# Four larger gaps of attention work per unit instead of eight, in a fused RWKV-7 and mixture-of-experts kernel

## The chip, the cores and the metric

One core of a Trainium2 chip. The metric is the device time of one execution in microseconds (us). The engines are called as in the profile: PE is TensorE's matmul, PEld its weight load, DVE VectorE, ACT ScalarE, POOL GpSimd, SP SyncE.

## The reference, cut to what matters

```python
# attention: batch 4, heads 8, 768 tokens, head size 40, float32
for t in range(S):
    y[:, :, t]  = einsum('bhd,bhde->bhe', r_t, state)
    Sa          = einsum('bhde,bhe->bhd', state, a_t)
    state       = state * w_t - einsum('bhd,bhe->bhde', Sa, b_t) + einsum('bhd,bhe->bhde', v_t, k_t)
# x = y as (3072 tokens, 320); then 4 experts of 320 -> 1024 -> 320
p = domain_probs / (domain_probs.sum(-1, keepdims=True) + 1e-9)
for e in range(4):
    out += p[:, e:e+1] * (relu(x @ w1[e]) @ w2[e])
```

## The kernel before

The kernel works on 24 units: one unit is 64 tokens of two batches with all 8 heads. The recurrence over tokens is turned into small matrices inside a unit. Four generators make the attention of a unit, and each `yield` is a place where the driver may put other work on TensorE: `within` (does not need the state: `pw`, `pg`, transposes of A, N, K, R, V, `pc`, `pf`, `pe`, `pev`), `substitute` (a triangular solve of 31 steps on GpSimd), `merge` (`pY`, `pQ`), and `step` (`prh`, `psn`, `psa`, `pst`, `px`, `prs`, `psd`, `py`). The mixture of a unit is four "ups" (`ph`) and four "downs" (`po`). An up contracts 320 features: two blocks of 128 rows and one of 64.

Two rings of PSUM banks matter: four banks for everything small, four for the mixture. A bank is a piece of the memory that TensorE writes, and it is written anew only after its last reader: in the kernel before, the third `psn` matmul starts at 633.91 us, 0.06 after the copy of `pQ` has ended (633.85). Four names besides those of the banks come back below: `gl` is the product of a unit's decays and reads `pw`, EV is the copy of `pev`, QTc is the result of the substitution, which `pY` needs, and `xT` is the input of the mixture, which a transfer brings from the result of `py`. The profile records a float32 matmul twice and a transpose once (18724 records: 9024 matmuls twice, 676 transposes once); the counts of matmuls below are counts of records.

```python
def big(name):
    return ps.tile([P, 512], FP32, name=name, tag="big", bufs=4)

def within(q):
    pw = by(turn("pw", tok(n["W"]))[:], L)                 # 4 transposes into one bank
    nc.scalar.copy(out=G[:, :, 1:L], in_=pw[:, :, 0:L - 1])
    nc.vector.tensor_tensor_scan(out=G[...], ...)          # running product of the decays
    nc.vector.tensor_tensor(out=q.gl[:], in0=pw[:, :, L - 1:L], in1=G[:, :, L - 1:L], op=ALU.mult)
    yield
    ... # pg; RT, VT, pc; AT, NT, KT; pf, pe; pev: a yield after each group

def up(e):
    ph = [ps.tile(..., tag="mm", bufs=4) for _ in range(2)]
    for f in range(NF):                # 128-row blocks first: 32 records
        for g in range(2): ...         # lhsT=w1_sb[:, e, g, ...], rhs=xT[:, g, :]
    for f in range(0, NF, 2):          # then the 64-row block: 16 records
        for i in range(2): ...         # lhsT=w1_last[...], rhs=xT[i * DT:(i + 1) * DT, 2, :]
    # Relu on ScalarE

for n, stages in enumerate(((before, s), (s,), (s,), (s, m, w), (w,), (w,), (w,), (w, m))):
    for gen in stages:
        next(gen, None)
    ...
    mix(1)                             # one up or one down after each of eight small gaps
```

The order of the program text is not quite the order on TensorE, because the framework's scheduler moves instructions: in the trace of the changed kernel unit 1's `pY` starts at 73.89 us, ahead of unit 0's first up (76.34), which the text has before it.

Of the kernel before, what the change touches and what calls it, by code (L numbers as in the profile page):

```python
# [15 lines left out]
def kernel(  # L16
# [51 lines left out]
    def big(name):  # L68
        return ps.tile([P, 512], FP32, name=name, tag="big", bufs=4)
# [203 lines left out]
    def within(q):  # L273
# [3 lines left out]
        q.G = G = sb.tile([P, 2 * NJ, L], FP32, name="G", tag="G", bufs=2)  # L277
# [6 lines left out]
        q.gl = sb.tile([P, 2 * NJ, 1], FP32, name="gl", tag="gl", bufs=3)  # L284
# [8 lines left out]
        nc.vector.reciprocal(out=gp[:], in_=gp[:])  # L293
        q.K, q.N = k_tok(), n_tok()
# [5 lines left out]

        def turned(name, x, keep=False):
            t = sb.tile([P, NJ, P], FP32, name=name, tag=name if keep else "turned", bufs=2)
            nc.scalar.copy(out=t[:].rearrange("p j t -> p (j t)"), in_=turn("p" + name, tok(x))[:])  # L303
            return t

        def causal_scores():
            q.RT = turned("RT", n["R"], True)
            VT = turned("VT", q.V)
            q.CT = causal(CTs(), quadrants("pc", BY_TOKENS, L, lambda j, s, i: (
                d_half(j, s), i, j, of_pairs(VT, d_half(j, s), j, i), of_pairs(q.RT, d_half(j, s), j, i),  # L310
            )))

        if not q.start:
            causal_scores()
# [5 lines left out]
        yield  # L320

# [11 lines left out]
        if q.start:  # L333
            causal_scores()
# [10 lines left out]
    def substitute(q, eng):  # L345

        blocks = sb.tile([P, H, Q], FP32, name="blocks", bufs=2)
# [158 lines left out]
    def mixture(q, xT):  # L506
# [4 lines left out]
        def up(e):  # L511
            ph = [ps.tile([P, NF // 2, P], FP32, name="ph", tag="mm", bufs=4) for _ in range(2)]

            for f in range(NF):
                for g in range(2):
                    nc.tensor.matmul(  # L516
                        out=ph[f % 2][:, f // 2, :], lhsT=w1_sb[:, e, g, f * P:(f + 1) * P],
                        rhs=xT[:, g, :], start=(g == 0 and f < 2), stop=False,
                    )
            for f in range(0, NF, 2):  # L520
                for i in range(2):
                    nc.tensor.matmul(  # L522
                        out=ph[i][:, f // 2, :], lhsT=w1_last[i * DT:(i + 1) * DT, e, f // 2, :],
                        rhs=xT[i * DT:(i + 1) * DT, 2, :], start=False, stop=(f == NF - 2),
                    )
            for i in range(2):
                h = sb.tile([P, NF // 2, P], FP32, name="hs", tag="hs", bufs=6)
                nc.scalar.activation(out=h[:], in_=ph[i][:], func=ACTF.Relu)  # L528
                hs[e, i] = h

        def down(e):
            po = ps.tile([P, DM], FP32, name="po", tag="mm", bufs=4)
            for f in range(NF):
                nc.tensor.matmul(  # L534
                    out=po[:], lhsT=hs[e, f % 2][:, f // 2, :], rhs=w2_sb[:, e, f, :],
                    start=(f == 0), stop=(f == NF - 1),
                )
            sc = gate[:, q.c, q.bp, e:e + 1]
            if e == 0:
                nc.vector.tensor_scalar(out=osb[:], in0=po[:], scalar1=sc, scalar2=None, op0=ALU.mult)  # L540
            else:
                nc.vector.scalar_tensor_tensor(  # L542
                    out=osb[:], in0=po[:], scalar=sc, in1=osb[:], op0=ALU.mult, op1=ALU.add,
                )

        up(0)
        yield
        for e in range(E):
            if e + 1 < E:
                up(e + 1)  # L550
                yield
            down(e)
            yield
        for i in range(2):
            row = q.b[i] * S + q.c * L
            nc.sync.dma_start(out=out[row:row + L, :], in_=osb[i * L:(i + 1) * L, :])

    work = []

    def mix(n):  # L560

        while n and work:
            try:
                next(work[0])
                n -= 1
            except StopIteration:
                work.pop(0)
# [10 lines left out]
    for u in (0, 1, 1, 1):  # L578
# [4 lines left out]
    m = merge(units[0])  # L583
    run(m, 2)
    for u in range(NU):
        q = units[u]
        xT = sb.tile([P, 3, P], FP32, name="xT", tag="xT", bufs=3)
        s = step(q, xT)
        w, before = iter(()), m
        more = u + 2 < NU  # L590
        if u + 1 < NU:
            m = merge(units[u + 1])
        if more:
            load(begin(u + 2), srcs)
            w = within(units[u + 2])
        for n, stages in enumerate(((before, s), (s,), (s,), (s, m, w), (w,), (w,), (w,), (w, m))):
            for gen in stages:
                next(gen, None)
                if u == 0 and n == 3 and gen is s:
                    for e in range(2, E):  # L600
                        load_expert(e)
                    run(z)
            if n == 3:
                work.append(mixture(q, xT))
            if n == 6 and more:
                run(substitute(units[u + 2], nc.gpsimd))
            if u or n % 2:
                mix(1)
    mix(-1)


# [26 lines left out]
```

## Time and profile before

| | before |
|---|---|
| time, median of 4 | 1244.37 us (1243.86 to 1245.14) |
| TensorE busy | 1197.9 us, 96% |
| next busiest | GpSimd, 41% |
| one unit in the steady part, `pw` to `pw` | 49.73 us (median of the trace) |
| units | 24 |

TensorE is full from the fourth slice on, so the time is a prologue plus some twenty equal units. The lines that show this stand in the prediction. This is the timeline of TensorE in the kernel before from the first up of unit 0; the columns are start, length, engine, line, operation, result and sources, array shape, operand shape, count, and in brackets an idle time and what ended it.

```profile
63.54 0.68 PE L516 MATMUL ph<-xT,w_sb 128*128 128x128 f32 x4
...
66.25 3.36 PE L516 MATMUL ph<-xT,w_sb 128*128 128x128 f32 x28 [0.71 <-DMA xT<-Y]
69.54 1.16 PE L522 MATMUL ph<-xT,w_last 64*128 64x128 f32 x16
...
72.97 0.70 PE L233 MATMUL pKT<-ident,k_tok 128*128 128x128 f32 x4 [1.79 <-DVE Z L366]
73.47 5.36 PE L516 MATMUL ph<-xT,w_sb 128*128 128x128 f32 x32
78.76 1.16 PE L522 MATMUL ph<-xT,w_last 64*128 64x128 f32 x16
...
83.25 0.69 PE L390 MATMUL pY<-QTc,F 32*32 32x32 f32 x32
```

The first up of unit 0 fills most of the time in which VectorE works on unit 1's substitution (its last Z ends at 73.0); the second follows, and `pY`, whose input QTc is ready at 74.3, comes only at 83.25.

### The profile page before, as it was taken

To read this page: it belongs to the slowest core of one execution; us is meant where nothing else is said; L and a number is where in the kernel's file an instruction comes from. 1 tells how busy PE (TensorE), PEld (TensorE's weight loads), DVE (VectorE), ACT (ScalarE), POOL (GpSimd) and SP (SyncE) were. 2 spreads that over 40 slices of the span, in tenths; PEclk is the share of its full clock that TensorE was granted. 3 is DMA by queue.
4 is the path that set the end of the run, shared out by engine and by line. 5 is a ranking of instruction groups with operands and counts; after the bars stand their busy time and mean duration, and the time that the engine had idled before them with its cause. 6 is when DMAs were issued, how large, how long until landed. Compare 5 with 4: busy or idle time off the path is not lost.

```text
span 1241.6 us, 42664 instructions
## 1 busy us (share of the span) xinstructions
PE 1197.9 (96%) x18724; PEld 1012.1 (82%) x18724; DVE 382.7 (31%) x790; ACT 319.6 (26%) x801; POOL 505.7 (41%) x1668
## 2 busy tenths in 40 slices
PE   5389999999999999999999999999999999999998
PEld 4378888888888888888888888888888888888886
DVE  5543143142231431422314314223143142231110
ACT  3122322222223222222232222222222222222111
POOL 4434634526426345264263452643634526436000
PEclk9699999999999999999999999999999999999999
DMA  5772220120211201202112012021120220000000
GB/s 97 173 199 49 35 45 13 35 45 9 40 30 18 46 13 35 44 10 39 26 23 45 12 36 42 11 40 24 24 45 12 36 42 11 14 14 2 13 13 6
DMA packets 179176, 45.55 MB, mean 37 GB/s; under 512 B 159488, under 2 KB 177968, under 8 KB 178992
## 3 DMA queue, kind: packets, MB, share of 16 engines
q1 hardware_dynamic: 177872, 42.66, 17.7%
q8 instruction: 148, 2.42, 0.8%
q10 hardware_dynamic: 1120, 0.16, 0.1%
q14 instruction: 36, 0.29, 0.1%
HBM read 34.13 MB, written 3.93 MB: 31 GB/s over the span
## 4 chain that ended last, share of the span: by engine, by line
PE 93%; DVE 2%; POOL 1%; ACT 1%; issue 1%; DMA 0%; SPq 0%; DVEq 0%; ACTq 0%; POOLq 0%
PE po L534 34%; PE ph L516 29%; PE ph L522 8%; PE py L260 2%; PE psd L260 2%; ACT QT L407 1%; PE pQ L402 1%; PE psa L260 1%; PE pY L390 1%; PE px L260 1%; PE psn L260 1%; PE pf L260 1%; PE pev L260 1%; PE pc L260 1%; PE pw L233 1%
## 5 line engine op out<-in xcount | busy, mean ns | idle before, releaser
L534 PE MATMUL po<-w_sb,hs 128*128 128x320 f32 x1536 | 440.2, 437 | 0.0
L534 PEld LDWEIGHTS po<-w_sb,hs 128*128 128x128 f32 x1536 | 282.5, 190 | 107.3
L516 PE MATMUL ph<-xT,w_sb 128*128 128x128 f32 x3072 | 367.7, 278 | 0.7 <-DMA xT<-Y 0.7
L516 PEld LDWEIGHTS ph<-xT,w_sb 128*128 128x128 f32 x3072 | 352.3, 193 | 6.3 <-DMA xT<-Y 0.9
L360 POOL TENSOR_TENSOR tmp<-M,Z 128x60 f32<-128x60 f32 (+24 forms) x713 | 196.3, 275 | 94.1 <-DVE M L353 40.1
L366 POOL TENSOR_TENSOR Z<-Z,tmp 128x60 f32<-128x60 f32 (+24 forms) x713 | 202.3, 284 | 55.8
L528 ACT ACTIVATE hs<-ph 128x512 f32<-128x512 f32 x192 | 104.2, 595 | 416.4 <-PE ph L522 416.4
L349 POOL COPY blocks<-F 32x256 f32<-32x256 f32 x92 | 36.2, 393 | 309.8 <-ACT F L327 306.9
L542 DVE SCALAR_TENSOR_TENSOR osb<-po,gate,osb 128x320 f32<-128x320 f32 x72 | 39.6, 551 | 335.0 <-PE po L534 335.0
L383 POOL COPY QT<-QTc 32x256 f32<-32x256 f32 x96 | 54.0, 563 | 185.7 <-DVE QTc L377 182.0
L522 PE MATMUL ph<-xT,w_last 64*128 64x128 f32 x1536 | 111.6, 285 | 0.0
L522 PEld LDWEIGHTS ph<-xT,w_last 64*128 64x128 f32 x1536 | 93.2, 187 | 11.6
L268 DVE COPY_PREDICATED TT<-mask_up,pe 128x256 f32<-128x256 int32 x48 | 18.6, 439 | 147.8 <-PE pe L260 147.8
L540 DVE TENSOR_SCALAR osb<-po,gate 128x320 f32<-128x320 f32 x24 | 13.2, 550 | 161.9 <-PE po L534 161.9
L462 ACT COPY RS<-prs 64x256 f32<-64x256 f32 x88 | 32.2, 366 | 103.2 <-PE prs L260 102.1
L353 DVE STREAM_TRANSPOSE M<-blocks 128x1024 f32<-128x1024 f32 x24 | 47.3, 1971 | 33.7 <-POOL blocks L349 33.7
L293 DVE RECIPROCAL gp<-gp 128x320 f32<-128x320 f32 x24 | 51.4, 2142 | 0.0
L476 DVE TENSOR_TENSOR state<-psd,state 128x160 f32<-128x160 f32 x44 | 12.2, 319 | 118.6 <-PE psd L260 118.6
L303 ACT COPY AT<-pAT 128x512 f32<-128x512 f32 x24 | 14.0, 585 | 110.6 <-PE pAT L233 110.6
L407 ACT COPY QT<-pQ 32x256 f32<-32x256 f32 x48 | 17.4, 362 | 85.5 <-PE pQ L402 85.2
L303 ACT COPY RT<-pRT 128x512 f32<-128x512 f32 x24 | 14.0, 585 | 80.6 <-PE pRT L233 80.6
L390 PE MATMUL pY<-QTc,F 32*32 32x32 f32 x768 | 17.0, 194 | 15.6 <-DVE QTc L377 15.6
(114 smaller groups left out, 1139.5 us busy)
## 6 DMA issues: line engine op xcount, KB each, us to landing
w_sb<-in_moe_w_dram SPq DMA_DIRECT2D x4, 1280.0 KB
w_sb<-in_moe_w_dram SPq DMA_DIRECT2D x8, 512.0 KB
natW<-in_w_dram SPq DMA_DIRECT2D x48, 80.0 KB
natA<-in_a_dram SPq DMA_DIRECT2D x48, 80.0 KB
natB<-in_b_dram SPq DMA_DIRECT2D x48, 80.0 KB
natK<-in_k_dram SPq DMA_DIRECT2D x48, 80.0 KB
out_dram<-osb SPq DMA_DIRECT2D x48, 80.0 KB
xT<-Y SPq DMA_DIRECT2D x168, 20.0 KB
```

Source lines behind the costliest of these rows:

```text
L260: nc.tensor.matmul(out=p[row][half(col), at * out_cols:(at + 1) * out_cols], lhsT=lhsT, rhs=rhs, start=(n == 0), stop=(n == len(terms) - 1),)
L293: nc.vector.reciprocal(out=gp[:], in_=gp[:])
L349: ins = eng.tensor_copy(out=blocks[quarter(i)], in_=q.F[quarter(i), :, quarter(i % 2)])
L353: nc.vector.transpose(out=M[:], in_=cols)
L360: ins = eng.tensor_tensor(out=t, in0=M[:, j:j + 1, j + 1:Q].to_broadcast([P, n, m]), in1=Z[:, 0:n, j:j + 1].to_broadcast([P, n, m]), op=AL ...
L366: eng.tensor_tensor(out=Z[:, 0:n, j + 1:Q], in0=Z[:, 0:n, j + 1:Q], in1=t, op=ALU.add)
L383: ins = nc.gpsimd.tensor_copy(out=q.QT[quarter(i), :, quarter(i % 2)], in_=QTc[quarter(i)])
L516: nc.tensor.matmul(out=ph[f % 2][:, f // 2, :], lhsT=w1_sb[:, e, g, f * P:(f + 1) * P], rhs=xT[:, g, :], start=(g == 0 and f < 2), stop=False,
L522: nc.tensor.matmul(out=ph[i][:, f // 2, :], lhsT=w1_last[i * DT:(i + 1) * DT, e, f // 2, :], rhs=xT[i * DT:(i + 1) * DT, 2, :], start=Fals ...
L528: nc.scalar.activation(out=h[:], in_=ph[i][:], func=ACTF.Relu)
L534: nc.tensor.matmul(out=po[:], lhsT=hs[e, f % 2][:, f // 2, :], rhs=w2_sb[:, e, f, :], start=(f == 0), stop=(f == NF - 1),)
L542: nc.vector.scalar_tensor_tensor(out=osb[:], in0=po[:], scalar=sc, in1=osb[:], op0=ALU.mult, op1=ALU.add,)
```

## The change

Its intent: fewer and larger gaps, each with its transposes first, so that TensorE changes its array shape less often; and mixture pieces of one up and one down whose 64-row blocks come first, directly after the 64-row matmuls of attention.

```diff
-        return ps.tile([P, 512], FP32, name=name, tag="big", bufs=4)
+        return ps.tile([P, 512], FP32, name=name, tag="big", bufs=5)
@@ within: RT and VT are transposed one gap earlier, pc one gap later; gl gets 4 buffers, G gets 3
@@ mixture
-            ph = [... tag="mm", bufs=4 ...]
-            (32 records of 128 rows, then 16 of 64 rows)
+            ph = [... tag="mm", bufs=3 ...]
+            for f in range(0, NF, 2):
+                for i in range(2):
+                    nc.tensor.matmul(..., lhsT=w1_last[...], rhs=xT[i * DT:(i + 1) * DT, 2, :],
+                                     start=(f == 0), stop=False)
+            for f in range(NF):
+                for g in range(2):
+                    nc.tensor.matmul(..., rhs=xT[:, g, :], start=False, stop=(g == 1 and f >= NF - 2))
@@ the pieces of a unit: up(0), the last unit's down(3), up(1), down(0), up(2), down(1), up(3), down(2)
@@ driver, for each unit u
-        for n, stages in enumerate(((before, s), (s,), (s,), (s, m, w), (w,), (w,), (w,), (w, m))): ...
+        share = 1 + (u > 1)
+        run(w, 1); run(w_next); run(s, 1)        # C: pw; pev; px, prs
+        mix(share)
+        run(w, 1); run(s)                        # D: pg, RT, VT; psd, py
+        if u:
+            mixture(q, q.xT)
+        run(w, 1); run(m, 1)
+        mix(share)
+        run(w, 2); run(m, 1); run(s_next, 1); run(m)   # A: AT, NT, KT; pc, pY, prh, psn, pQ
+        mix(share)
+        run(w, 1); run(s_next, 1)                # B: pf, pe, psa, pst
+        mix(2 if u else 1)
```

A piece is one up or one down.

More of the change, by code (lines that the diff above doesn't have):

```diff
@@ L276, in within @@
         pw = by(turn("pw", tok(n["W"]))[:], L)
-        q.G = G = sb.tile([P, 2 * NJ, L], FP32, name="G", tag="G", bufs=2)
+        q.G = G = sb.tile([P, 2 * NJ, L], FP32, name="G", tag="G", bufs=3)
         nc.vector.memset(G[:, :, 0:1], 0.0)
@@ L283, in within @@
         )
-        q.gl = sb.tile([P, 2 * NJ, 1], FP32, name="gl", tag="gl", bufs=3)
+        q.gl = sb.tile([P, 2 * NJ, 1], FP32, name="gl", tag="gl", bufs=4)
         nc.vector.tensor_tensor(out=q.gl[:], in0=pw[:, :, L - 1:L], in1=G[:, :, L - 1:L], op=ALU.mult)
@@ L293, in within, with turned, turn_rv, causal_scores @@
         nc.vector.reciprocal(out=gp[:], in_=gp[:])
+        def turned(name, x, keep=False):
+            t = sb.tile([P, NJ, P], FP32, name=name, tag=name if keep else "turned", bufs=2 if keep else 3)
+            nc.scalar.copy(out=t[:].rearrange("p j t -> p (j t)"), in_=turn("p" + name, tok(x))[:])
+            return t
+        def turn_rv():
+            q.RT = turned("RT", n["R"], True)
+            return turned("VT", n["V"])
+        def causal_scores(VT):
+            q.CT = causal(CTs(), quadrants("pc", BY_TOKENS, L, lambda j, s, i: (
+                d_half(j, s), i, j, of_pairs(VT, d_half(j, s), j, i), of_pairs(q.RT, d_half(j, s), j, i),
+            )))
+        if not q.start:
+            VT = turn_rv()
+            yield
         q.K, q.N = k_tok(), n_tok()
@@ L299, in within @@
         q.V = n["V"]
-        def turned(name, x, keep=False):
-            t = sb.tile([P, NJ, P], FP32, name=name, tag=name if keep else "turned", bufs=2)
-            nc.scalar.copy(out=t[:].rearrange("p j t -> p (j t)"), in_=turn("p" + name, tok(x))[:])
-            return t
-        def causal_scores():
-            q.RT = turned("RT", n["R"], True)
-            VT = turned("VT", q.V)
-            q.CT = causal(CTs(), quadrants("pc", BY_TOKENS, L, lambda j, s, i: (
-                d_half(j, s), i, j, of_pairs(VT, d_half(j, s), j, i), of_pairs(q.RT, d_half(j, s), j, i),
-            )))
-        if not q.start:
-            causal_scores()
         yield
@@ L320, in within @@
         yield
+        if not q.start:
+            causal_scores(VT)
+            yield
         pf = quadrants("pf", BY_TOKENS, L, lambda j, s, i: (
@@ L333, in within @@
         if q.start:
-            causal_scores()
+            causal_scores(turn_rv())
+            yield
         q.EV = EVs()
@@ L345, in substitute @@
     def substitute(q, eng):
-        blocks = sb.tile([P, H, Q], FP32, name="blocks", bufs=2)
+        blocks = sb.tile([P, H, Q], FP32, name="blocks")
         for i in range(P // Q):
@@ L511, in up @@
         def up(e):
-            ph = [ps.tile([P, NF // 2, P], FP32, name="ph", tag="mm", bufs=4) for _ in range(2)]
+            ph = [ps.tile([P, NF // 2, P], FP32, name="ph", tag="mm", bufs=3) for _ in range(2)]
+            for f in range(0, NF, 2):
+                for i in range(2):
+                    nc.tensor.matmul(
+                        out=ph[i][:, f // 2, :], lhsT=w1_last[i * DT:(i + 1) * DT, e, f // 2, :],
+                        rhs=xT[i * DT:(i + 1) * DT, 2, :], start=(f == 0), stop=False,
+                    )
             for f in range(NF):
@@ L517, in up @@
                         out=ph[f % 2][:, f // 2, :], lhsT=w1_sb[:, e, g, f * P:(f + 1) * P],
-                        rhs=xT[:, g, :], start=(g == 0 and f < 2), stop=False,
-                    )
-            for f in range(0, NF, 2):
-                for i in range(2):
-                    nc.tensor.matmul(
-                        out=ph[i][:, f // 2, :], lhsT=w1_last[i * DT:(i + 1) * DT, e, f // 2, :],
-                        rhs=xT[i * DT:(i + 1) * DT, 2, :], start=False, stop=(f == NF - 2),
+                        rhs=xT[:, g, :], start=False, stop=(g == 1 and f >= NF - 2),
                     )
@@ L531, in down @@
         def down(e):
-            po = ps.tile([P, DM], FP32, name="po", tag="mm", bufs=4)
+            po = ps.tile([P, DM], FP32, name="po", tag="mm", bufs=3)
             for f in range(NF):
@@ L544, in down, with store @@
                 )
-        up(0)
-        yield
-        for e in range(E):
-            if e + 1 < E:
-                up(e + 1)
-                yield
-            down(e)
-            yield
-        for i in range(2):
-            row = q.b[i] * S + q.c * L
-            nc.sync.dma_start(out=out[row:row + L, :], in_=osb[i * L:(i + 1) * L, :])
-    work = []
-    def mix(n):
-        while n and work:
-            try:
-                next(work[0])
-                n -= 1
-            except StopIteration:
-                work.pop(0)
+        def store():
+            for i in range(2):
+                row = q.b[i] * S + q.c * L
+                nc.sync.dma_start(out=out[row:row + L, :], in_=osb[i * L:(i + 1) * L, :])
+        todo.append(lambda: up(0))
+        if last:
+            todo.append(last.pop())
+        for e in range(1, E):
+            todo.append(lambda e=e: up(e))
+            todo.append(lambda e=e: down(e - 1))
+        last.append(lambda: (down(E - 1), store()))
+    todo, last = [], []
+    def mix(n):
+        for piece in todo[:n]:
+            piece()
+        del todo[:n]
     def run(gen, n=99):
@@ L577 @@
     run(substitute(units[0], nc.gpsimd))
-    for u in (0, 1, 1, 1):
+    for u in (0, 0, 1, 1, 1):
         next(ws[u])
@@ L582, with begin_step @@
     next(z)
-    m = merge(units[0])
-    run(m, 2)
+    run(merge(units[0]))
+    def begin_step(u):
+        units[u].xT = sb.tile([P, 3, P], FP32, name="xT", tag="xT", bufs=2)
+        return step(units[u], units[u].xT)
+    s = begin_step(0)
+    run(s, 2)
+    w_next = ws[1]
     for u in range(NU):
         q = units[u]
-        xT = sb.tile([P, 3, P], FP32, name="xT", tag="xT", bufs=3)
-        s = step(q, xT)
-        w, before = iter(()), m
-        more = u + 2 < NU
+        m = s_next = w = iter(())
         if u + 1 < NU:
-            m = merge(units[u + 1])
-        if more:
+            m, s_next = merge(units[u + 1]), begin_step(u + 1)
+        if u + 2 < NU:
             load(begin(u + 2), srcs)
             w = within(units[u + 2])
-        for n, stages in enumerate(((before, s), (s,), (s,), (s, m, w), (w,), (w,), (w,), (w, m))):
-            for gen in stages:
-                next(gen, None)
-                if u == 0 and n == 3 and gen is s:
-                    for e in range(2, E):
-                        load_expert(e)
-                    run(z)
-            if n == 3:
-                work.append(mixture(q, xT))
-            if n == 6 and more:
-                run(substitute(units[u + 2], nc.gpsimd))
-            if u or n % 2:
-                mix(1)
-    mix(-1)
+        if u == 0:
+            run(s)
+            for e in range(2, E):
+                load_expert(e)
+            run(z)
+            mixture(q, q.xT)
+        share = 1 + (u > 1)
+        run(w, 1)
+        run(w_next)
+        run(s, 1)
+        mix(share)
+        run(w, 1)
+        run(s)
+        if u:
+            mixture(q, q.xT)
+        run(w, 1)
+        run(m, 1)
+        mix(share)
+        run(w, 2)
+        run(m, 1)
+        run(s_next, 1)
+        run(m)
+        mix(share)
+        run(w, 1)
+        run(s_next, 1)
+        if u + 2 < NU:
+            run(substitute(units[u + 2], nc.gpsimd))
+        mix(2 if u else 1)
+        s, w_next = s_next, w
+    mix(len(todo))
+    last.pop()()
 _INS = ["r", "k", "v", "w", "a", "b", "moe_domain_probs", "moe_w1", "moe_w2"]
```

## The prediction

> **What bounds the kernel now.** I read the page's busy table first, then its 40 slices, the chain that ended last, the waits of TensorE, and last a timeline of TensorE over one unit.
>
> ```profile
> PE 1197.9 (96%) x18724; PEld 1012.1 (82%) x18724; DVE 382.7 (31%) x790; ACT 319.6 (26%) x801; POOL 505.7 (41%) x1668
> ...
> PE   5389999999999999999999999999999999999998
> ...
> PE 93%; DVE 2%; POOL 1%; ACT 1%; issue 1%; DMA 0%; SPq 0%; DVEq 0%; ACTq 0%; POOLq 0%
> ...
> PE pY L390 <- DVE QTc L377: 15.6, 1, 15.6
> ```
>
> TensorE is never idle after the third slice, the last chain is TensorE for 93%, and its longest wait happens once, in the prologue. Nothing else is above 41%. So outside the first 75 us the time is the sum of TensorE's start-to-start times, and a change pays only if that sum shrinks. Busy time cannot show this[...], so I work with the starts. In the chain in order of time the same `po` starts at 180.30 and again at 230.03, and in the unit timeline the same `pw` at 603.38 and 653.12: one unit takes 49.74 us, and there are 24.
>
> ```profile
> 603.38 0.66 PE L233 MATMUL pw<-ident,natW 128*128 128x128 f32 x4
> 603.88 4.47 PE L534 MATMUL po<-w_sb,hs 128*128 128x320 f32 x16
> 608.19 0.60 PE L233 MATMUL pg<-ident,G 128*128 128x128 f32 x4
> ...
> 614.63 0.60 PE L233 MATMUL pAT<-ident,a_tok 128*128 128x128 f32 x4
> ...
> 615.94 3.74 PE L516 MATMUL ph<-xT,w_sb 128*128 128x128 f32 x32
> 619.60 1.16 PE L522 MATMUL ph<-xT,w_last 64*128 64x128 f32 x16
> 620.70 0.69 PE L260 MATMUL pf<-NT,AT 64*64 64x64 f32 x32
> 621.21 0.65 PE L260 MATMUL pe<-AT,KT 64*64 64x64 f32 x32
> 621.79 3.84 PE L516 MATMUL ph<-xT,w_sb 128*128 128x128 f32 x32
> 625.56 1.16 PE L522 MATMUL ph<-xT,w_last 64*128 64x128 f32 x16
> ...
> 627.88 4.57 PE L534 MATMUL po<-w_sb,hs 128*128 128x320 f32 x16
> 632.38 0.69 PE L402 MATMUL pQ<-Yq,Qc 32*32 32x32 f32 x32
> 633.00 0.68 PE L260 MATMUL prh<-state,AT 64*64 64x40 f32 x32
> 633.49 1.11 PE L260 MATMUL psn<-ident,state 64*64 64x64 f32 x32
> 634.53 3.84 PE L516 MATMUL ph<-xT,w_sb 128*128 128x128 f32 x32
> ```
>
> The column that matters is the first; `64*64` and the like is the array shape. The same `po` of 16 takes 4.31 us between two neighbours of its own shape (603.88 to 608.19) and 4.50 between two of another (627.88 to 632.38). `ph` takes 3.66 after transposes of its shape and 3.77 after 64*64. So a change of shape costs about 0.10 when it is left and another 0.10 when 128 columns are entered (0.02 to 0.05 for 64 or 32 columns, from the first starts of `pf` and `pev`). `psn` takes 1.04 where its equal `pe` takes 0.58: 0.46 us of a real wait each unit, for the bank of `pQ`, whose copy ends at 633.85 (with four banks in the ring; its third matmul starts at 633.91).
>
> [...]
>
> **The change, part by part.** No matmul is added or removed; the totals per kind stay. I took the new order of TensorE from the built program and call the four gaps A (transposes AT, NT, KT; pc, pY, prh, psn, pQ), B (pf, pe, psa, pst), C (pw; pev, px, prs) and D (pg, RT, VT; psd, py), each followed by `ph` 64-row, `ph`, `po`.
>
> Shape changes: 20 a unit before, 15 after (A six, B, C and D three each). Each new stretch priced from the starts above:
> - A: 12 transposes 1.31 plus exit 0.09; pc 0.62; pY 0.62; prh 0.49; psn 0.58 (no wait now: pQ comes after it, and a fifth bank); pQ 0.62: 4.33.
> - B: pf 0.51; pe and psa 0.47 each (0.58 less its exit of 0.11); pst 0.56: 2.01.
> - C: pw 0.44 plus exit 0.09; pev 0.49; px 0.47; prs 0.58: 2.07.
> - D: 1.31 plus 0.09; psd and py 2.21 (650.91 to 653.12): 3.61.
> - mixture, four times: 1.09, then `ph` 3.77 less its exit 0.09, then `po` 4.31: 9.08 each, 36.32. One exit of `po` into B: 0.09.
>
> Sum 48.43, so 1.31 us less per unit than 49.74: 0.85 from shape changes, 0.46 from the wait of `psn`. Over some 22 units 29 us, or 2.3%. That is the gain if nothing new waits.
>
> What is new: a larger gap asks for many banks within 2 us, with no 4 us `po` between for others to empty them. I resolved the semaphores of the built program. In B, the second `psa` matmul stream needs `pf`'s first bank (copy on ScalarE) and `pst` needs `pe`'s (VectorE): about 0.13 and 0.10 late, 0.23 together. In A everything is in time: `pQ` starts at 3.7 after A's start, its `Yq` copies end at about 3.5. In C it is not. The ring of five goes pw, pev, pev, px, px, and then prs takes the banks of `pw` and of the first `pev`. The semaphore that prs's second bank waits for is that of `gl`, the last reader of `pw`, and `gl` stands behind the scan:
>
> ```profile
> 605.92 1.18 DVE L280 TENSOR_TENSOR_SCAN G<-G,first 128x512 f32<-128x512 f32 x1
> 607.21 0.17 DVE L285 TENSOR_TENSOR gl<-pw,G 128x8 f32<-128x8 f32 x1
> ...
> 615.26 0.59 ACT L303 COPY AT<-pAT 128x512 f32<-128x512 f32 x1 [4.93 <-PE pAT L233]
> ```
>
> From the start of pw: copy of G starts after 0.63 (as AT: 614.63 to 615.26); the scan 0.61 later (9.59 and 10.20 in the prologue's timeline); `gl` ends 1.46 after the scan's start (605.92 to 607.38); 0.06 to release. That is 2.76. prs would want its second bank at 0.53 + 0.49 + 0.47 + 0.01 = 1.50. So TensorE stands for 1.26 us in C, every unit from 2 to 21. In the kernel before the same `gl` harmed nothing, since `po` followed pw.
>
> New unit: 48.43 + 1.26 + 0.23 = 49.92 us, 0.18 more than before. Twenty units: +3.6 us; the last two units have no pw, keep a few fewer changes of shape and lose psn's wait: -1.5.
>
> Prologue: in the kernel before, `ph` of unit 0 starts at 63.5 as soon as xT has landed, and its first two ups are done by 79.85 although VectorE works on unit 1's substitution until 73. In the new order the first `ph` stands behind unit 1's pY (and one pQ), which needs QTc, the end of that substitution, at about 73.7. Then pY, two copies of Yq, pQ: `ph` at about 76, partly at the half clock[...] (a stretch of `ph` at 0.213 instead of 0.112 stands at 73.5 already). Two ups end at about 87 to 88. It has pY and pev done by then, which leaves a loss of about 6 us (an estimate).
>
> Total: +3.6 - 1.5 + 6 = +8.1 on the span, so 1244.4 + 8 = 1252; I take 1251.
>
> **Rivals.** First, the five banks are enough and only the shape changes count: 22 x 1.08 us less (1.31 less B's 0.23) and the prologue's loss make about -18, so 1226. For it: the change was made for this, and the ring was widened. Against it: the semaphore on `gl`, which is in the program, and scan, copy and `gl` have measured lengths. Second, entering the 64-row blocks straight from 64*64 is cheaper than from 128*128, perhaps 0.1 to 0.2 in each of four gaps: -10 to -18 us, about 1237. Against it: [...] (last start of `ph` L522 to `pf` 0.20 against 0.10 inside). Third, GpSimd's substitution becomes the bound, since pY now comes sooner after pf: pf to the last Z takes 27.7 us (620.70 to 648.4), and in the new order B, C, D and the start of A give about 37; so it is hidden, with some 8 us in hand. If it were not, each unit would wait on QTc and the time would pass 1270. Fourth, one set of `ph` banks and one of `po` (three instead of four): Relu (1.08 us for two) has the 4.3 us of `po`, the eviction of `po` (0.55) a whole gap; hidden.
>
> **Range and chances.** The sizes of the shape changes are good to about 0.15 us a unit, the wait in C to 0.2, B to 0.1, together about 0.3 x 20 = 6 us; the prologue to 3. So 1251 with 1240 to 1260 for 8 in 10; the low side is wider because the second rival is there. Faster by over 2% needs under 1219.5, which even the first rival misses: 0.06. Slower by over 2% needs over 1269.3, a wait of which I have no sign: 0.06.
>
> **What would show it.** Right: in the unit timeline prs starts about 2.7 us after pw and holds TensorE for about 1.2 us, released by VectorE's `gl`; psn takes 0.58; `po` takes 4.31 in three gaps of four; the period is near 49.9; the first `ph` starts near 76. Wrong: a period near 48.6 with prs 1.5 after pw (first rival); the 64-row `ph` blocks taking about 0.95 instead of 1.09 (second); a wait of pY on QTc in steady units (third).

## More of the kernel before

The granted clock was 1.00 from 60 to 66 us, 0.50 from 74 to 76 and 1.00 from 80 to 90.

## The result, and the profile after

| | before | after |
|---|---|---|
| time, median of 4 each | 1244.37 us | 1277.45 us (1274.83 to 1280.18) |
| ratio | | 1.0266 (95%: 1.0236 to 1.0295), slower |
| unit, `pw` to `pw`, median | 49.73 us | 50.24 us |
| TensorE busy | 1197.9 us | 1196.3 us |

Ratios here are the mean time of one kernel's runs over that of the other's of the same rounds, so they are not quite the ratio of the medians. The four runs of the changed kernel fall on two levels, near 1275 and near 1280; the profiled one is at 1275.01. I have not found what makes the two levels; differences of 2 or 3 us against its median should not be read.

The page of the changed kernel: TensorE's busy time, its share in the slices, the granted clock, the engines of the chain that ended last, and then TensorE's waits (engine, what waited, releaser: total us, times, longest).

```profile
PE 1196.3 (94%) x18724; PEld 1016.3 (80%) x18724; DVE 385.1 (30%) x790; ACT 326.6 (26%) x801; POOL 509.2 (40%) x1668
...
PE   5377999999999999999999999999999999999998
...
PEclk9678999999999999999999999999999999999999
...
PE 88%; DVE 4%; POOL 3%; issue 2%; ACT 1%; DMA 0%; SPq 0%; DVEq 0%; POOLq 0%; ACTq 0%
```

```profile
PE pY L398 <- DVE QTc L385: 30.9, 3, 17.9
PE prs L260 <- DVE gl L285: 10.2, 20, 0.5
PE prs L260 <- ACT EV L350: 8.1, 21, 0.4
...
PE pQ L410 <- issue: 3.3, 3, 1.2
```

Three things are new. The third and fourth slices are at 7 with the clock at 7 and 8. `prs` waits 20 times. And TensorE stands three times at `pQ` for nothing that the profile shows ("issue"). The 17.9 of `pY` is unit 0's own, which the kernel before has too (15.6); the other two waits of `pY` are new.

To divide the loss I take the start of `psa` in each unit, which both kernels have once a unit, and correct it for the mixture pieces done by then (4.67 us an up, 4.31 a down, close to their starts in both traces). The delay against before is then 7.4 us at unit 1, 15.5 at unit 2, 30.8 at unit 22, and 31.5 at the end of the span (1273.1 against 1241.6 us). Of the 15.3 between units 2 and 22, five large steps (1.59, 1.90, 0.99, 1.41, 1.93) hold 5.3 above a plain one of 0.51; the rest, 10.0, is twenty steps of 0.50 in the mean. Four of the five hold one of TensorE's waits for "issue" (three at `pQ`, one at `ph`). The fifth (0.99) holds a hole of the same kind that shows only 0.14 us of idle time, in the 64-row `ph` at 580.2; it stands four units before the one at 781.27. So:

| part | predicted | measured |
|---|---|---|
| prologue, up to `psa` of unit 2 | +6 | +15.5 |
| twenty steady units | 20 x 0.18 = +3.6 | 20 x 0.50 = +10.0 |
| five stalls without a releaser | not foreseen | +5.3 |
| the last two units | -1.5 | +0.8 |
| sum | +8.1 | +31.6, of 31.5 on the span |

The steady unit of the changed kernel, TensorE, gap C with the gap that follows:

```profile
600.47 0.60 PE L233 MATMUL pw<-ident,natW 128*128 128x128 f32 x4
601.00 0.68 PE L260 MATMUL pev<-natV,TT 64*64 64x40 f32 x32
601.49 0.67 PE L260 MATMUL px<-RT,SaT 64*64 64x64 f32 x32
602.55 0.33 PE L260 MATMUL prs<-RT,SN 64*64 64x64 f32 x4 [0.39 <-ACT EV L350]
603.40 0.68 PE L260 MATMUL prs<-RT,SN 64*64 64x64 f32 x28 [0.52 <-DVE gl L285]
604.01 1.16 PE L524 MATMUL ph<-xT,w_last 64*128 64x128 f32 x16
605.10 3.84 PE L530 MATMUL ph<-xT,w_sb 128*128 128x128 f32 x32
608.77 4.47 PE L542 MATMUL po<-w_sb,hs 128*128 128x320 f32 x16
613.09 0.60 PE L233 MATMUL pg<-ident,G 128*128 128x128 f32 x4
```

And VectorE in the same microseconds:

```profile
601.72 1.35 DVE L280 TENSOR_TENSOR_SCAN G<-G,first 128x512 f32<-128x512 f32 x1 [0.50 <-ACT G L279]
603.18 0.17 DVE L285 TENSOR_TENSOR gl<-pw,G 128x8 f32<-128x8 f32 x1
```

C takes 604.01 - 600.47 = 3.54 us, and `po` before `pg` takes 4.31 (608.77 to 613.09), as in a gap of its own shape. The scan lasts 1.35 us where it lasted 1.18 before. ScalarE's copies of `pev` start at the same 601.72, but they are not what makes it longer: in the run with the 64-row blocks last the scan runs beside the same four copies and takes 1.22. Another difference from the kernel before is what GpSimd does meanwhile: there it copies QT (a copy at 606.12 of 1.16 us, beside the scan from 605.92), here it is in the operations of the substitution (one at 601.69 of 0.30 us, one at 602.07 of 1.09). The cause was not tested.

The prologue of the changed kernel, TensorE:

```profile
66.10 1.13 PE L260 MATMUL pc<-RT,VT 64*64 64x64 f32 x32
73.89 1.06 PE L398 MATMUL pY<-QTc,F 32*32 32x32 f32 x32 [6.65 <-DVE QTc L385]
...
76.34 2.67 PE L524 MATMUL ph<-xT,w_last 64*128 64x128 f32 x16
78.94 5.56 PE L530 MATMUL ph<-xT,w_sb 128*128 128x128 f32 x32
...
94.66 0.62 PE L260 MATMUL pf<-NT,AT 64*64 64x64 f32 x26
...
117.54 0.69 PE L260 MATMUL pc<-RT,VT 64*64 64x64 f32 x32
124.58 1.06 PE L398 MATMUL pY<-QTc,F 32*32 32x32 f32 x32 [6.35 <-DVE QTc L385]
...
128.49 5.49 PE L542 MATMUL po<-w_sb,hs 128*128 128x320 f32 x16
```

TensorE stands twice, at 67 to 74 and at 118 to 124.6. After each stand it works more slowly for a few microseconds: a 64-row `ph` group takes 2.60 instead of 1.09, `po` 5.41 instead of 4.40. The granted clock, at 7 and 8 tenths in these slices, was 0.50 from 66 to 82 us and from 121 to 130, and 1.00 from 84 to 95 and from 134 to 140. What lowers it was not tested.

### The profile page after: what moved, and what is told of

It is laid out like the page before. It is cut to its first block, busy times and chain, and to the rows that moved or that the text cites. A ratio compares the mean times of both kernels' runs of the same rounds, so it can differ in the third digit from the quotient of the medians. Undisturbed runs are those within 1.5% of the kernel's fastest.

```text
span 1273.1 us, 42628 instructions
## 1 busy us (share of the span) xinstructions
PE 1196.3 (94%) x18724; PEld 1016.3 (80%) x18724; DVE 385.1 (30%) x790; ACT 326.6 (26%) x801; POOL 509.2 (40%) x1668
## 3 DMA queue, kind: packets, MB, share of 16 engines
q8 instruction: 147, 2.41, 0.8%
## 4 chain that ended last, share of the span: by engine, by line
PE 88%; DVE 4%; POOL 3%; issue 2%; ACT 1%; DMA 0%; SPq 0%; DVEq 0%; POOLq 0%; ACTq 0%
PE po L542 32%; PE ph L530 28%; PE ph L524 8%; DVE G L280 2%; PE py L260 2%; PE psd L260 2%; POOL tmp L368 1%; POOL Z L374 1%; PE psa L260 1%; PE pQ L410 1%; PE pY L398 1%; PE prs L260 1%; PE pf L260 1%; PE prh L260 1%; PE pc L260 1%
## 5 line engine op out<-in xcount | busy, mean ns | idle before, releaser
L542 PE MATMUL po<-w_sb,hs 128*128 128x320 f32 x1536 | 430.4, 433 | 0.0
L368 POOL TENSOR_TENSOR tmp<-M,Z 128x60 f32<-128x60 f32 (+24 forms) x713 | 213.4, 299 | 94.2 <-DVE M L361 40.2
L374 POOL TENSOR_TENSOR Z<-Z,tmp 128x60 f32<-128x60 f32 (+24 forms) x713 | 205.0, 288 | 55.8
L391 POOL COPY QT<-QTc 32x256 f32<-32x256 f32 x96 | 37.7, 393 | 101.7 <-DVE QTc L385 94.1
L398 PEld LDWEIGHTS pY<-QTc,F 32*32 32x32 f32 x768 | 15.1, 113 | 33.0 <-issue 31.7
L334 ACT COPY F<-pf 128x256 f32<-128x256 f32 x48 | 15.6, 375 | 97.4 <-PE pf L260 97.4
L260 PE MATMUL prs<-RT,SN 64*64 64x64 f32 x704 | 21.9, 227 | 18.2 <-DVE gl L285 10.2
L280 DVE TENSOR_TENSOR_SCAN G<-G,first 128x512 f32<-128x512 f32 x24 | 31.8, 1326 | 18.5 <-ACT G L279 18.3
```

The lines of the kernel that those rows point to most:

```text
L260: nc.tensor.matmul(out=p[row][half(col), at * out_cols:(at + 1) * out_cols], lhsT=lhsT, rhs=rhs, start=(n == 0), stop=(n == len(terms) - 1),)
L280: nc.vector.tensor_tensor_scan(out=G[:].rearrange("p c i -> p (c i)"), data0=G[:].rearrange("p c i -> p (c i)"), data1=first[:].rearrange( ...
L368: ins = eng.tensor_tensor(out=t, in0=M[:, j:j + 1, j + 1:Q].to_broadcast([P, n, m]), in1=Z[:, 0:n, j:j + 1].to_broadcast([P, n, m]), op=AL ...
L374: eng.tensor_tensor(out=Z[:, 0:n, j + 1:Q], in0=Z[:, 0:n, j + 1:Q], in1=t, op=ALU.add)
L398: nc.tensor.matmul(out=py[quarter(i - 1), h * Q:(h + 1) * Q], lhsT=q.F[quarter(i), h, 0:Q], rhs=QTc[quarter(i), h, :], start=True, stop=True,)
L542: nc.tensor.matmul(out=po[:], lhsT=hs[e, f % 2][:, f // 2, :], rhs=w2_sb[:, e, f, :], start=(f == 0), stop=(f == NF - 1),)
```

## The experiments

My theory after reading the traces: the loss has three separate sources. (1) The prologue: the first ups stand behind unit 1's `pY`, and then unit 2's `pY` comes before GpSimd's substitution has ended. (2) In C the ring of five banks makes `prs` wait for the last readers of `pw` (`gl`) and `pev` (EV). (3) The stalls without a releaser, which I took to come from TensorE's instruction stream. Rivals: the order of blocks in an up costs time by itself; the number of pieces per gap is at fault; the stalls come from something else than the instruction stream. All ten kernels of the experiments computed the right result. Their summary:

| kernel | time, us | ratio to before | unit, us | delay at `psa` of unit 2 |
|---|---|---|---|---|
| before | 1244.4 | 1 | 49.73 | 0 |
| after | 1277.45 | 1.0266 | 50.24 | 15.5 |
| first ups before `pY` | 1270.26 | 1.0216 | 50.12 | 13.1 |
| two pieces per gap in unit 1 | 1336.15 | 1.0725 | 51.8 and 54.2 in turn | 15.9 |
| `gl` off the bank of `pw` | 1259.03 | 1.0115 | 49.40 | 16.4 |
| `pev` moved to D | 1253.02 | 1.0068 | 48.89 | 16.3 |
| one piece moved in the prologue | 1269.30 | 1.0205 | 50.24 | 9.0 |
| after, 64-row blocks last | 1276.88 | 1.0260 | 50.90 | 3.2 |
| before, 64-row blocks first | 1284.66 | 1.0323 | 50.85 | 11.6 |
| three edits, first version | 1243.07 | 0.9990 | 49.25 | 3.4 |
| three edits, second version | 1237.08 | 0.9937 | 48.89 | 2.5 |
| instruction stream shifted | 1273.90 | 1.0243 | 50.24 | 15.1 |

### The first ups ahead of pY

```diff
-            nc.tensor.transpose(out=p[:, j * P:(j + 1) * P], in_=src(j), identity=ident[:])
+            ins = nc.tensor.transpose(out=p[:, j * P:(j + 1) * P], in_=src(j), identity=ident[:])
+            if name == "pAT" and j == 0:
+                tc.keep_in_program_order(ins)
```

> Changed kernel with one pin: the transposes AT of each gap A may not be issued before the mixture pieces written ahead of them, so unit 0's first two ups run before unit 1's pY. Theory (the prologue order costs: pY waits 6.65 us for unit 1's substitution with the ups behind it, then runs at the half clock): the first ph starts near 66 instead of 76.3, the wait of 6.65 us on QTc goes, the time falls by 8 to 11 us to about 1267. Rival (the idle stretch only moves, because the next pY waits for GpSimd's substitution anyway): the later wait on QTc grows by as much and the time stays within 2 us of 1277. Steady units unchanged at 50.25 us under both.

Measured: 1270.26 us (1269.72 to 1273.47), 1.0216 (1.0199 to 1.0233). The delay at unit 1 fell from 7.4 to 3.3, so this half of the prologue is what it was thought to be, but smaller than expected: the first `ph` now stands for its own input.

```profile
PE pY L400 <- DVE QTc L387: 24.2, 2, 17.6
...
PE ph L526 <- DMA xT<-Y: 6.7, 1, 6.7
```

One of the two new waits of `pY` (24.2 - 17.6 = 6.6) remains, and the step from unit 1 to unit 2 grew from 8.1 to 9.7. So there is a second half with another cause, and the rival named in the expectation holds in part: at unit 2 only 2.4 us of the gain are left. The rest of the 5.3 us between the two profiled runs came in the steady units, which was not expected: there the scan took 1.22 us in most units instead of 1.35, and the unit is 50.12 instead of 50.24.

### Two pieces in two of unit 1's gaps

```diff
-        mix(share)                  # after C
+        mix(1 + (u > 0))
@@
-        mix(share)                  # after A
+        mix(1 + (u > 0))
```

> Changed kernel with unit 1's first and third gap given two mixture pieces instead of one (nothing else). Theory (in unit 1 the gaps are short, so pf to pY is shorter than GpSimd's 27 us): the wait of 6.35 us of the second steady pY on QTc falls to about 2 us or less, the slow-clock stretch after it goes too (2.6 us), the time falls by 5 to 8 us to about 1271. Rival (the wait is made by something else, as a late start of the substitution): the wait stays near 6 us and the time within 2 us of 1277. Steady units 50.25 under both.

Measured: 1336.15 us (1327.69 to 1338.69), 1.0725. A clear miss. The wait of unit 2's `pY` did fall (from `pc` to `pY` it is 2.65 us instead of 7.04), but the mixture now runs two pieces, that is one gap, ahead in every unit that follows: the first up of a unit comes in gap A instead of B, one gap after the `py` whose result it reads, and waits for the transfer.

```profile
PE ph L524 <- DMA xT<-Y: 31.9, 35, 2.9
```

The lesson is that the queue of pieces has a memory: a piece more, early, moves every later piece.

### One piece moved instead of added

```diff
-        share = 1 + (u > 1)
+        shares = ((1, 1, 0, 1), (2, 1, 1, 2))[u] if u < 2 else (2, 2, 2, 2)
         # gap C: shares[0], D: shares[1], A: shares[2], B: shares[3]
```

> Changed kernel with one mixture piece moved from unit 0's gap A to unit 1's first gap, so the mixture keeps its phase against the attention in all later units (the earlier trial with more pieces in unit 1 let the mixture run one piece ahead, so that ups met xT still in flight). Theory (unit 1's single-piece gaps are shorter than GpSimd's substitution): the 6.35 us wait of the second pY on QTc falls to 1 to 3 us, its half-clock stretch shrinks, no wait on xT in steady units, steady unit 50.25; time lower by 4 to 8 us, about 1271. Rival (the idle only moves to the gap that lost its piece): time within 2 us of 1277.

Measured: 1269.30 us (1267.77 to 1270.53), 1.0205 (1.0189 to 1.0221). The step from unit 1 to unit 2 fell from 8.1 to 1.5 and the steady unit stayed at 50.24. Unit 2's `pY` waits 1.69 us instead of 6.35:

```profile
120.56 0.69 PE L398 MATMUL pY<-QTc,F 32*32 32x32 f32 x32 [1.69 <-DVE QTc L385]
```

So the second half of the prologue is the wait of unit 2's `pY` on GpSimd's substitution, and it is there because unit 1's gaps have one piece each. By the trace of the changed kernel: `pf` at 94.66, the transposes that follow the substitution start at 123.35, which is 28.7 us; `pc` ends at about 118.2, only 23.6 us after `pf`. The difference of 5.1 and the 1.1 us of those two transposes (the second ends at 124.4) are 6.2 of the wait's 6.35 us.

### gl taken off the bank of pw

```diff
         nc.scalar.copy(out=G[:, :, 1:L], in_=pw[:, :, 0:L - 1])
+        wl = sb.tile([P, 2 * NJ, 1], FP32, name="wl", tag="wl", bufs=2)
+        nc.scalar.copy(out=wl[:], in_=pw[:, :, L - 1:L])
...
-        nc.vector.tensor_tensor(out=q.gl[:], in0=pw[:, :, L - 1:L], in1=G[:, :, L - 1:L], op=ALU.mult)
+        nc.vector.tensor_tensor(out=q.gl[:], in0=wl[:], in1=G[:, :, L - 1:L], op=ALU.mult)
```

> Changed kernel with the last column of pw copied to SBUF by ScalarE right after the copy of G, so gl no longer reads the bank of pw and the scan no longer holds it. Theory (prs waits first for EV on pev's bank, then for gl on pw's): the second of the two waits in gap C goes (0.73 to about 0), the first grows by the extra copy (0.57 to about 0.75), gap C falls from 3.54 to about 2.9, a steady unit from 50.25 to about 49.6, the time by 12 to 15 us to about 1263. Rival (the wait is for the slow scan's own sake or EV alone sets it): unit within 0.2 us of 50.25, time within 4 us of 1277.

Measured: 1259.03 us (1257.63 to 1259.70), 1.0115 (1.0100 to 1.0130). The unit is 49.40. The wait on `gl` is gone. The one on EV was expected to grow (0.57 to 0.75) and did not: it costs 0.6 us, C takes 2.70 where 2.9 was expected, and the gain is larger than forecast. TensorE in C:

```profile
594.14 0.67 PE L260 MATMUL px<-RT,SaT 64*64 64x64 f32 x32
594.64 0.30 PE L260 MATMUL prs<-RT,SN 64*64 64x64 f32 x4
595.21 0.68 PE L260 MATMUL prs<-RT,SN 64*64 64x64 f32 x28 [0.27 <-ACT EV L352]
595.82 1.16 PE L526 MATMUL ph<-xT,w_last 64*128 64x128 f32 x16
```

Twenty units of 50.24 - 49.40 = 0.84 are 16.8 us, and the time fell by 18.4. So the bank of `pw`, held until `gl`, turns a gain of 0.33 us a unit (49.73 to 49.40) into a loss of 0.51. It is not all that stands between the changed kernel and the gain that was hoped for: the wait on EV is still there.

### pev moved from C to D

```diff
         run(w, 1)
-        run(w_next)
         run(s, 1)
         mix(share)

         run(w, 1)
+        run(w_next)
         run(s)
```

> Changed kernel with pev moved from gap C to gap D (after the transposes, before psd), so C asks for five banks (pw, px, px, prs, prs) and the ring has five. Theory (the ring of five banks is what gap C lacks): no wait of prs at all, gap C 1.65, gap D longer by about 0.5 to 0.6, a steady unit near 49.0, the time lower by 22 to 27 us, about 1252. Rival (waits move to gap D, where psd or py wait for the banks of the transposes and pev): unit at 49.7 or more, gain under 12 us.

Measured: 1253.02 us (1252.14 to 1253.60), 1.0068 (1.0053 to 1.0083). Two banks fewer are asked for in C and no wait is left there:

```profile
590.77 0.60 PE L233 MATMUL pw<-ident,natW 128*128 128x128 f32 x4
591.30 0.69 PE L260 MATMUL px<-RT,SaT 64*64 64x64 f32 x32
591.81 0.65 PE L260 MATMUL prs<-RT,SN 64*64 64x64 f32 x32
592.39 1.16 PE L524 MATMUL ph<-xT,w_last 64*128 64x128 f32 x16
```

The unit is 48.89, 0.84 less than before: the intent of the change, at last. What is left of the loss is the prologue (16.3) and more of the stalls without a releaser (six at `ph` and `pQ` besides these), now at `py` too, in the gap that has grown:

```profile
PE py L260 <- issue: 2.7, 4, 1.1
```

### The order of blocks in an up, both ways

First the changed kernel with the old order (128-row blocks first):

```diff
-            (64-row blocks, start=(f == 0), stop=False; then 128-row blocks, start=False, stop=(g == 1 and f >= NF - 2))
+            (128-row blocks, start=(g == 0 and f < 2), stop=False; then 64-row blocks, start=False, stop=(f == NF - 2))
```

> Changed kernel with the old order inside an up: 128-row blocks first, 64-row last. If the order saves one change of shape per gap, each gap costs about 0.2 us more: 64*64 to 128 (0.21), 128 to 64*128 (0.20), 64*128 to 128 (0.20) instead of two changes and none; a steady unit 51.05 instead of 50.25, +17 us over the steady units. Against that the prologue: 128-row blocks need only the first parts of xT, the ups are no longer scheduled behind unit 1's pY, as with the pin -7 us. Together about 1287. Rival (entering the 64-row blocks from 64*64 is as dear as the old way, the order saves nothing): unit at 50.25 and time at 1270.

Measured: 1276.88 us (1275.07 to 1277.24), 1.0260 (1.0246 to 1.0274): the same as the changed kernel. Both halves of the expectation's reasoning show, but not in its sizes, and in the sum they cancel. The steady unit is 50.90, 0.66 worse, which is some 13 us (17 expected). C is 0.13 shorter than in the changed kernel, since the scan takes 1.22 here; without that the order costs 0.79, close to the 0.8 expected. The prologue is 12.3 us better (3.2 instead of 15.5; 7 expected): the 128-row blocks need only the parts of the input that land first (in the changed kernel's trace unit 0's eight transfers for them have landed by 65.9 us, the four for the 64-row blocks by 69.0), and the scheduler puts the ups of unit 0 ahead of `pY` again:

```profile
76.93 1.16 PE L530 MATMUL ph<-xT,w_last 64*128 64x128 f32 x16
...
78.52 0.69 PE L398 MATMUL pY<-QTc,F 32*32 32x32 f32 x32
```

The new order gains in the steady part and loses about as much in the prologue.

Then the kernel before with the new order, the same exchange the other way round.

> Kernel before with only the 64-row blocks put first in each up, everything else as before. Three of the four ups follow and precede 64*64 work, where both orders make three changes; the one after the transposes gains one change (0.2 us). Theory: a unit of 49.9 to 50.0 instead of 49.74, time 1247 to 1251, so this part pays only with an up and a down together. Rival (64*64 to 64*128 is a cheap change): a unit near 49.2, time near 1232.

Measured: 1284.66 us (1282.82 to 1285.32), 1.0323 (1.0309 to 1.0337). A miss. In the kernel before, the first up of a unit comes soon after `py`, and the 64-row blocks read the part of the input that arrives last (in the trace of the kernel before, unit 0's four transfers for them land from 67.0 to 69.3 us, the eight others by 66.2):

```profile
PE ph L516 <- DMA xT<-Y: 14.6, 29, 2.1
```

So the block order is not good or bad by itself: it needs a gap between `py` and the first up, which the four larger gaps have and the eight small ones have not (29 waits and 14.6 us on `xT` here, none in the changed kernel's list of TensorE's waits).

### The three edits together, first version

The piece moved in the prologue (as above), the order in C turned round, and a dependency without a semaphore that keeps a unit's `pY` behind the last up issued (shortened here).

```diff
-        run(w, 1); run(w_next); run(s, 1)        # pw; pev; px, prs
+        run(s, 1); run(w_next); run(w, 1)        # px, prs; pev; pw
@@ merge, at the first matmul of pY
+                if h == 0 and i == 1 and ups:
+                    tc.add_manual_dep(ins.ins, ups[-1].ins.name, <no semaphore>, reason="behind the last up")
```

> Changed kernel with three repairs: gap C in the order px, prs, pev, pw (no bank of the ring is asked for while gl, the scan or EV hold it), unit 1's pY may not pass unit 0's first two ups, and one piece moved from unit 0 to unit 1. Theory: prs without a wait, gap C 2.1 to 2.2 instead of 3.54, a steady unit of 48.9 to 49.0 instead of 50.25; the first ph near 66 to 68; the time about 1237, 1230 to 1243, so faster than the kernel before by 0.1 to 1.1 per cent. What may stay: [...]0.3 us of psa's wait for F's copy in gap B per unit. Rival (the four-gap order is bound by something else than these waits): unit at 49.7 or more, time over 1245.

Measured: 1243.07 us (1241.76 to 1243.43), 0.9990 (0.9977 to 1.0002): no different from before. The prologue came out as wanted (3.4), but the unit is 49.25 and not 48.9: with `px` first, `pev` waits for the bank of `px`, which VectorE empties (in the changed kernel its two operations on `px` take 0.77 us together, from 603.26). That wait is about 0.4 us a unit, an estimate from the units: 49.25 against 48.89 with `pev` in D. Turning the order round moved the wait.

### The three edits together, second version

`pev` in D, the piece moved in the prologue, and the old block order for unit 0 alone.

```diff
+            if q.u == 0:
+                (128-row blocks, start=(g == 0 and f < 2); then 64-row blocks, stop=(f == NF - 2))
+            else:
                 (64-row blocks, start=(f == 0); then 128-row blocks, stop=(g == 1 and f >= NF - 2))
```

> The changed kernel with pev moved from C to D, unit 0's two ups alone in the old order (128-row blocks first), and one piece moved from unit 0's gap A to unit 1's first gap. My account is that the loss has three terms: the prologue (15.5 us), the wait of prs in C (about 0.5 us a unit against before)[...]. This kernel takes away the first two and leaves the third: unit period 48.9 (as where pev alone was moved), prologue +1 to +4 against before at psa of unit 2 instead of +16, no prs wait, stalls of 5 to 8 us left. Time about 1239, between 1234 and 1244, the fastest of all. Rival: the gains of the two edits do not add (ups scheduled early make unit 1's gaps wait for xT, or the second wait of pY on QTc stays as long as it was because GpSimd's substitution is what ends it): then prologue +8 or more and 1247 or more.

Measured: 1237.08 us (1235.11 to 1237.56, 5 runs), 0.9937 (0.9925 to 0.9950). The fastest of all, 0.6% below before. Unit 48.89, delay at unit 2 of 2.5, no wait of `prs`, and `pY` waits once only, for unit 0:

```profile
PE pY L398 <- DVE QTc L385: 17.9, 1, 17.9
...
PE py L260 <- issue: 2.9, 3, 1.4
```

So the first two sources are settled: with them away, their time is away. By the steps, the twenty units give 20 x 0.84 = 16.8 and the prologue costs 2.5, which would make -14.3; the span came out 6.25 us shorter than before. The 8 us between stand in a handful of larger steps. Six stalls without a releaser in the steady part (0.68, 1.06, 0.37, 0.58, 1.43 and 0.77 us of idle time) make 4.9 of them. Idle time shows them too short: where I compare the starts of TensorE's matmuls with those of the median unit, these six cost 6.2 us (the last of them read from its unit's step), and four more that show less than 0.3 us of idle time (at 147.8, 555.3, 689.3 and 814.1 us) cost 1.6. Together that is 7.8 of the 8 us.

### The instruction stream shifted

The four stalls with a recorded wait stood in the changed kernel at 224.98, 426.95, 781.27 and 982.58 us (the last start before each). This edit puts 32 more transposes into a long idle stretch of the prologue, with the same result as the first four.

```diff
-        for e in range(E):
+        for e in [e for e in range(E) for _ in range(9)]:
             nc.tensor.transpose(out=pp[:, e * n:(e + 1) * n], in_=flat[:, :, e], identity=ident[0:n, 0:n])
```

> The changed kernel with the 4 transposes of the probabilities issued 9 times instead of once, into the same place, in TensorE's long idle stretch before the first pY: 32 more matmuls in the stream (128 more load and multiply instructions), no other change. If the four stalls without a releaser (at 224.98, 426.95, 781.27 and 982.58 us in the changed kernel) come from instruction fetch in blocks of 256, they keep their position modulo 256 in TensorE's stream, so they must move by half a block: since a unit is about 68 over a multiple of 256 that is two units or 100 us away, to pQ or the first 64-row ph near 326, 529, 680 to 730 and 880 to 932 us, and the four old places run without a stall. If they come from something in time or in the data[...], they stay at the same matmuls. Time the same within 0.3% of the changed kernel either way: 1275, between 1272 and 1281.

Measured: 1273.90 us (1273.09 to 1276.85), 1.0243 (1.0227 to 1.0259). The stalls moved, and the old places run without one, but not by half a block: by a quarter. My arithmetic was wrong there. A transpose runs as one pass, a load and a multiply, so 32 of them are 64 instructions and not 128 (18724 matmul records for 9700 matmuls of the program, 676 of them transposes, show which kind runs twice). A steady unit is 1600 instructions, 64 more than six blocks of 256, so the stalls should move by one unit. They do: from 224.98 to 174.37, from 426.95 to 376.18, from 781.27 to 729.42 and from 982.58 to 930.32. TensorE, the changed kernel and then the shifted one:

```profile
224.52 0.66 PE L410 MATMUL pQ<-Yq,Qc 32*32 32x32 f32 x29
226.05 0.25 PE L410 MATMUL pQ<-Yq,Qc 32*32 32x32 f32 x3 [0.88 <-issue]
```

```profile
173.88 0.69 PE L410 MATMUL pQ<-Yq,Qc 32*32 32x32 f32 x31
175.32 0.21 PE L410 MATMUL pQ<-Yq,Qc 32*32 32x32 f32 x1 [0.76 <-issue]
...
225.07 0.69 PE L410 MATMUL pQ<-Yq,Qc 32*32 32x32 f32 x32
225.69 1.16 PE L524 MATMUL ph<-xT,w_last 64*128 64x128 f32 x16
```

I counted TensorE's instructions in the built programs (four for a matmul of two passes, two for a transpose, one for a semaphore instruction). All 23 stalls of this kind over 0.3 us in four kernels (4 in the changed one, 4 in the shifted one, 9 with `pev` in D, 6 in the fastest) stand at the 195th place of a block of 256; the records of TensorE in the traces, counted in order of start, give the same place for each, and for the fifth stall of the changed kernel too. The blocks of 256 are an estimate from the page of the changed kernel: 147 packets and 2.41 MB in the instruction queue, about 16.4 KB each, and TensorE's 37768 instructions over 147 packets are 257 to a packet.

```profile
q8 instruction: 147, 2.41, 0.8%
```

So the stalls belong to the instruction stream and its blocks. Not every block stalls: those that do lie in or right after dense stretches of short matmuls (A, and D once `pev` is in it), and the kernel before, whose dense stretches are shorter (`psd` and `py`: 128 records in 2.21 us, where A has 172 in 4.37), has none: between 140 and 1141 us no matmul of it starts 0.1 us later after the one before it than in the median unit. That TensorE stands there for the fetch of instructions was my assumption; the runs show the place of the stalls, not what it stands for.

## Why the prediction was wrong

It said 1251 with 1240 to 1260; the median is 1277.45. It saw that the kernel becomes slower, but by a quarter of the loss that came. By its own steps:

- **Shape changes: right.** `psn` takes 0.60, A 4.37 (4.33 predicted), D 3.57 (3.61), the four mixture pairs 36.40 (36.41 with the exit of `po`); `po` takes 4.31 in three gaps of four. With the wait in C gone the unit is 48.89; the prediction's sum without C's wait was 48.66.
- **The wait of prs on gl: right in mechanism, short in size.** "TensorE stands for 1.26 us in C": the second bank came 2.93 us after `pw`, not 2.76, because the scan ran 1.35 and not 1.18. C took 3.54 instead of 3.33, B 2.37 instead of 2.24. Together with A and D that makes a unit of 50.24 instead of 49.92, and 20 x 0.50 in place of 20 x 0.18: 6.4 us. The value of 1.18 was read in another place of the unit, and a scan's length was taken to be the same everywhere; related runs show 1.22 and 1.35.
- **The prologue: the step that failed most.** "Which leaves a loss of about 6 us (an estimate)" is 7.4 for the part it describes. But the third rival, GpSimd's substitution as the bound, was set aside with "B, C, D and the start of A give about 37; so it is hidden, with some 8 us in hand". That is true of units with two pieces per gap. In the first units a gap has one piece, the room is 23.6 us, and 8.1 us were lost there. Moving one piece took the step to 1.5.
- **Stalls without a releaser: not in the prediction at all.** Five of them, 5.3 us. The kernel before has none, so no line of its profile pointed to them; the density of A (172 records of matmuls and transposes in 4.4 us) was the only hint.
- **The last two units: wrong sign, small.** "-1.5" was +0.8: the pieces of one up and one down leave every `po` there for another shape (4.40 each), where the kernel before had two `po` in a row.
- **First rival (1226):** fell as stated, since the bank of `pw` was not in time; but with `pev` moved and the prologue mended the steady unit comes within 0.3 us of what that rival supposed (48.43 + 0.23), and the time to 1237. **Second rival (cheaper entry into the 64-row blocks):** wrong, 1.09 us as before. **Fourth (mixture banks):** hidden, as said.

Still open: the two levels of the changed kernel's runs (1275 and 1280), what sets the length of the scan, what lowers the granted clock, and why one block stalls and another at the same place of a later unit does not.

## What to carry to other kernels

Judge a reordering in the steady part and in the first units separately: a check that a background engine is "hidden" must be done with the work per gap that the first units really have. When gaps are merged, list for each bank of the ring its last reader and when it ends, since the work that used to lie between is gone; moving one group that needs banks to another gap took the unit from 50.24 to 48.89 us here, with the ring as it was. And when an engine stands for nothing that the profile shows, look at its place in the instruction stream: here 23 such stalls in four kernels, 0.3 to 1.4 us of idle time each, stood at the 195th of 256 instructions.
